# Another order of all work: r in pair loads turned on TensorE, keys of two chunks per DMA transpose, w spread by one load

## The chip, the cores and the metric

The kernel runs on one core of one Trainium2 chip. The metric is the device time of one execution in microseconds. The engines are called as in the profile: PE (TensorE, with PEld for its weight loads), DVE (VectorE), ACT (ScalarE), POOL (GpSimd) and SP (SyncE, which here only issues DMAs).

## The reference

An RWKV-5 style linear attention, followed by a layer norm and a feed-forward block with a residual. Shapes: batch 4, 8 heads, 768 tokens, head size 48; after attention the heads are put side by side to 384 channels, and the feed-forward is 384 to 1536 to 384.

```
for t in range(S):                       # per batch and head
    cur   = outer(u * k[t], v[t])
    y[t]  = r[t] @ (state + cur)
    state = w[:, None] * state + outer(k[t], v[t])
x   = y with the heads side by side       # (4, 768, 384)
xn  = (x - mean(x)) / sqrt(var(x) + 1e-6) * g_ln
out = x + relu(xn @ w_ch1) @ w_ch2
```

## The kernel before

**Tiling.** The 4 x 768 tokens are 24 chunks of 128 tokens, six to a batch. A chunk's attention is done in matrix form: keys are multiplied by a falling power of w (`Fk`) and queries by a rising one (`Fr`), so that `AT` (scores), a mask `AM`, `Y` (output) and `S` (state update, and the u term through q = r times k) are matmuls. The powers are exponentials of position times log w. `ZU`/`ZD` carry the state from chunk to chunk. The feed-forward (`UP`, `RL`, `DN`, `OT`) is matmuls of 128 channels with weights kept in SBUF; chunks are taken in the `GROUPS` of one or two.

**Layout.** Chunks 0 to 3 are loaded as two pairs: partition p then holds tokens 2p and 2p+1 of 256 tokens, and the pair steps (`LK2`, `LR2`, `LV2`, `SK2`, `SR2`, `AT2`, `AM2`, `Q2`, `CC2`, `VB2`, `Y2`) work on both. Chunks 4 to 23 are loaded one by one (`LK`, `LR`, `LV`) and use the plain steps. `AT` needs k and r with the channels on partitions, so every chunk's scaled k and r (tile `sc`) is turned: on PE through one PSUM bank named `tr` and an eviction (`TR`, `TC`) for chunks 0 to 7, by DMA transposes on SP (`TD`) for chunks 8 to 23. The normed x is turned on PE (`LT`, `XT`) for groups 0 to 7 and by DMA (`LTD`) for groups 8 to 17.

**Order.** Nothing is scheduled automatically. A hand-kept list, `PLAN`, names every step with its index and its engine (v DVE, s ACT, g POOL, - for PE or SP); each engine takes its instructions in this order, and waits where its operand is not ready. PSUM has one bank (or pair of banks) each for `tr`, `at`, `s`, `y` and `o`, and two named `hp` for `UP`. `RL` evicts `hp` on ACT or DVE.

**Steps that matter here.** `WF` loads w as a row, `LN` takes its logarithm, `WBM` spreads it over 128 partitions by a matmul, `FK2`, `FR2`, `FK`, `FR` are exponentials from it. `ROWS` loads u and w a second time by channel, for `UW` and `WL`. `DU` issues matmuls on a zero tile. `TL` is one line:

```
nc.scalar.preload_act_table_set("natural_log_exp_and_others")
```

`RS` computes 1/sqrt(variance) of a group: on ACT as Ln and then Exp, on POOL with a power. `SQ`, the squares, precedes it on ACT. In `PLAN` of before, `TL,0,s` stands among the first steps, ahead of `LN`; nine `RS` are on ACT and nine on POOL.

Of the kernel before, what the change touches and what calls it, by code (L numbers as in the profile page):

```python
# [14 lines left out]
ZPE = [1, 2, 3, 4]  # L15
SLOTS = {'kf': 8, 'rf': 8, 'vf': 10, 'sc': 6, 'vv': 6, 'trs': 6, 'q': 3, 'A': 3, 'cc': 6, 'Z': 4, 'ZS': 3, 'Vb': 4, 'x': 12, 'xn': 3, 'xT': 4, 'hT': 4, 'ot': 4}
PAIRS = 2
PLAN = """
MW,0,v LG,0,s LR,4,- MO,0,v MP,3,g MI2,0,g MZ,0,v ROWS,3,s WF,0,- LK2,1,- MP,4,g ROWS,1,s MM,0,g LK2,0,- TL,0,s MP,1,g MP,0,g MI,0,g LR2,0,- MM2,0,g
LN,0,s UGC,0,s ROWS,2,s DU,3504,- WBM,0,- ROWS,0,s LV2,0,- FK2,0,s LR2,1,- FK2,1,s FR2,1,s SK2,0,v FR2,0,s LV2,1,- SR2,0,v DU,4832,- TRk2,0,- TCk2,0,v LK,4,- UW,0,g  # L20
MP,2,v DU,1936,- TRr2,0,- SK2,1,v TCr2,0,s LR,5,- SR2,1,v CV2,0,s DU,2736,- AT2,1,- Q2,0,v LW1,2,- TRr2,1,- CV2,1,s AM2,1,v S,0,- LW1,1,- WL,0,s TCr2,1,v DU,704,-
AT2,0,- LK,5,- FK,0,s CC2,0,v ZU,0,v LV,4,- TRk2,1,- FR,0,s AM2,0,v S,1,- TCk2,1,s VB2,0,v DU,816,- Y2,0,- Q2,1,v AT2,2,- X,0,v SW,6,s SW,7,g AM2,2,v
SW,8,s DU,656,- Y2,1,- SR,4,g XN,0,s LK,6,- ZU,1,v SK,4,g LT,0,- S,2,- XT,0,v SW,4,s LW1,0,- MP,5,v X,1,v SQ,0,s SK,5,g AT2,3,- ZU,2,v LR,6,-
# [36 lines left out]


@with_exitstack
def kernel(
    ctx: ExitStack,
    tc: tile.TileContext,
    r: bass.AP,
    k: bass.AP,
    v: bass.AP,
    w: bass.AP,
    u: bass.AP,  # L70
# [187 lines left out]
    def MP(i, e):  # L258
        engines[e].memset(sc(i)[:, :, :, D:DP], 0.0)
# [525 lines left out]
```

## Time and profile before

| What | Value |
|---|---|
| median of 3 runs | 155.34 us (155.19 to 159.82) |
| profiled execution, its span | 155.5 us |
| PE busy | 143.6 us (92%) |
| DVE busy | 119.8 us (77%) |
| ACT busy | 78.7 us (51%) |
| POOL busy | 71.4 us (46%) |
| DMA queue of SP, share of 16 engines | 83.4% |

Busy times add up the instructions of an engine. An engine that is busy for most of the span can be the one that paces the kernel, but only a look at stretches and at waits says where. The granted TensorE clock is 0.998 of full speed in the mean. A row of a view of groups gives the busy time and the mean duration of one instruction, then the idle time ahead of the group and what ended it.

### The profile page before, as it was taken

The page shows a single profiled execution, that of the slowest core. Times are in us where ns is not written, and L with a number is a line of the kernel's source. Part 1 is how long each engine was busy: PE and PEld are TensorE (multiplying, and loading weights), DVE is VectorE, ACT ScalarE, POOL GpSimd, SP SyncE. Part 2 cuts the span into 40 slices and gives each one's busy share as a digit, 9 for nine tenths or more (in the row PEclk, how much of TensorE's full clock was granted, in tenths as well). Part 3 has the DMA queues.
Part 4 walks back from the last instruction along what each step waited for, and adds up shares of the span by engine and source line. Part 5 has one row for each costly group of instructions (what it writes and reads, how often), then busy time and mean ns, then how long its engine had stood idle before and what let it go on. Part 6 is the DMA issues. An engine that isn't in the chain of part 4 may idle for free.

```text
span 155.5 us, 4587 instructions
## 1 busy us (share of the span) xinstructions
PE 143.6 (92%) x1872; PEld 110.4 (71%) x1872; DVE 119.8 (77%) x229; ACT 78.7 (51%) x178; POOL 71.4 (46%) x109
## 2 busy tenths in 40 slices
PE   6989999989899868999999799899999799999991
PEld 2347888877776856788777578586777587868881
DVE  2289998549979769999995996899867539998532
ACT  3629678584361507539734457446066372146510
POOL 7220759481525547844589455332024413431500
PEclk9999999999999999999999999999999999999999
DMA  4999999998789999769999999899999998661503
GB/s 85 301 314 299 268 251 181 169 208 175 149 110 188 183 211 227 155 127 226 152 223 209 129 208 226 149 206 211 118 250 196 117 262 158 177 146 30 177 27 125
DMA packets 98486, 28.48 MB, mean 183 GB/s; under 512 B 93729, under 2 KB 96930, under 8 KB 98466
## 3 DMA queue, kind: packets, MB, share of 16 engines
q1 hardware_dynamic: 96802, 27.01, 83.4%
q0 software_dynamic: 432, 1.18, 4.1%
q8 instruction: 14, 0.23, 0.6%
q10 hardware_dynamic: 1232, 0.00, 0.4%
q14 instruction: 6, 0.05, 0.1%
HBM read 18.88 MB, written 4.72 MB: 152 GB/s over the span
## 4 chain that ended last, share of the span: by engine, by line
PE 41%; DMA 27%; DVE 12%; SPq 9%; issue 5%; POOL 3%; ACT 1%; DVEq 0%; POOLq 0%; ACTq 0%
PE o L676 17%; PE hp L648 17%; DMA trs<-sc 9%; DMA kf<-in_k_dram 5%; DMA w_sb<-in_moe_w_ch_dram 5%; DMA xT<-xn 3%; DVE Vb L567 3%; SPq L337 2%; DVE A L517 2%; DMA out_dram<-ot 2%; DMA rf<-in_r_dram 2%; SPq L356 2%; PE at L507 2%; POOL q L196 1%; DVE q L196 1%
## 5 line engine op out<-in xcount | busy, mean ns | idle before, releaser
L648 PE MATMUL hp<-xT,w_sb 128*128 128x128 bf16 (+1 forms) x648 | 56.1, 238 | 2.4 <-DMA xT<-xn 0.9
L648 PEld LDWEIGHTS <-w_sb 128*128 128x128 bf16 x648 | 48.8, 114 | 6.7 <-issue 2.7
L664 ACT ACTIVATE hT<-hp 128x512 bf16<-128x512 f32 x55 | 32.3, 592 | 41.7 <-PE hp L648 41.3
L676 PE MATMUL o<-w_sb,hT 128*128 128x384 bf16 x276 | 52.6, 326 | 0.6 <-DMA w_sb<-in_moe_w_ch_dram 0.4
L676 PEld LDWEIGHTS <-hT 128*128 128x128 bf16 x276 | 25.0, 97 | 13.9 <-issue 0.7
L517 DVE TENSOR_TENSOR A<-at,mask 128x1024 bf16<-128x1024 f32 x20 | 24.3, 1216 | 1.1 <-PE at L507 1.0
L608 POOL TENSOR_SCALAR xn<-x,sm 128x384 bf16<-128x384 f32 x14 | 9.0, 646 | 24.9 <-DVE x L592 16.1
L732 DVE SCALAR_TENSOR_TENSOR ot<-o,rs,x 128x384 f32<-128x384 f32 x23 | 14.1, 613 | 6.6 <-PE o L676 5.4
L196 POOL TENSOR_TENSOR sc<-kf,Fk 128x384 bf16<-128x384 f32 x14 | 15.3, 1100 | 4.7 <-DMA kf<-in_k_dram 4.7
L599 ACT ACTIVATE sqj<-x,sm 128x384 bf16<-128x384 f32 x24 | 14.6, 610 | 3.9 <-DVE x L592 3.8
L196 POOL TENSOR_TENSOR sc<-rf,Fr 128x384 bf16<-128x384 f32 x10 | 10.4, 1042 | 12.1 <-DMA rf<-in_r_dram 12.1
L592 DVE SCALAR_TENSOR_TENSOR x<-y,Vb 128x384 f32<-128x384 f32 x24 | 13.2, 550 | 2.4 <-POOL Vb L567 1.3
L666 DVE TENSOR_SCALAR hT<-hp 128x512 bf16<-128x512 f32 x17 | 11.5, 685 | 2.5 <-PE hp L648 2.4
L567 DVE TENSOR_TENSOR Vb<-vf,cc 128x384 f32<-128x384 f32 x13 | 11.4, 875 | 0.5 <-ACT cc L191 0.4
L196 POOL TENSOR_TENSOR q<-trs 128x512 bf16<-128x512 bf16 x8 | 9.4, 1170 | 3.4 <-DMA trs<-sc 1.8
L196 DVE TENSOR_TENSOR sc<-rf,Fr 128x384 bf16<-128x384 f32 (+1 forms) x12 | 8.2, 683 | 2.9 <-DMA rf<-in_r_dram 2.9
L196 DVE TENSOR_TENSOR sc<-kf,Fk 128x384 bf16<-128x384 f32 (+1 forms) x8 | 6.2, 780 | 5.1 <-DMA kf<-in_k_dram 5.1
L507 PE MATMUL at<-trs 48*128 48x128 bf16 x160 | 8.0, 219 | 2.3 <-DMA trs<-sc 2.3
L567 POOL TENSOR_TENSOR Vb<-vf,cc 128x384 f32<-128x384 f32 x7 | 5.8, 828 | 9.1 <-DVE cc L193 5.3
L271 PE MATMUL o<-warm 128*128 128x512 bf16 x26 | 8.1, 439 | 1.2 <-DVE u_p L210 1.2
L191 ACT CAST vv<-vf 128x384 bf16<-128x384 f32 (+1 forms) x15 | 8.1, 550 | 1.9 <-DMA vf<-in_v_dram 1.9
L507 PEld LDWEIGHTS <-trs 48*128 48x128 bf16 x160 | 4.5, 94 | 6.2 <-DMA trs<-sc 2.9
(98 smaller groups left out, 189.1 us busy)
## 6 DMA issues: line engine op xcount, KB each, us to landing
out_dram<-ot SPq DMA_DIRECT2D x23, 192.0 KB, 2.9
rf<-in_r_dram SPq DMA_DIRECT2D x20, 192.0 KB, 4.0
kf<-in_k_dram SPq DMA_DIRECT2D x20, 192.0 KB, 4.2
vf<-in_v_dram SPq DMA_DIRECT2D x20, 192.0 KB, 4.0
w_f<-in_moe_w_ch_dram SPq DMA_DIRECT2D x3, 768.0 KB, 6.0
w_sb<-in_moe_w_ch_dram POOLq DMA_DIRECT2D x3, 384.0 KB, 7.6
kf<-in_k_dram SPq DMA_DIRECT2D x2, 384.0 KB, 4.1
rf<-in_r_dram SPq DMA_DIRECT2D x2, 384.0 KB, 4.4
```

The source lines that it names most:

```text
L196: engines[e].tensor_tensor(out=out, in0=in0, in1=in1, op=ALU.mult)
L507: nc.tensor.matmul(out=t[:, par, q, :], lhsT=trs(i)[p0 : p0 + D, 1, q, :], rhs=trs(i)[p0 : p0 + D, 0, q, :], start=True, stop=True,)
L517: nc.vector.tensor_tensor(out=AA(i)[:, a:b].rearrange("p e q t -> p (e q) t"), in0=psum["at", i][:, a:b].rearrange("p e q t -> p (e q) t") ...
L567: engines[e].tensor_tensor(out=heads(Vb(i)), in0=vf(i), in1=cc(i)[:].unsqueeze(2).to_broadcast([P, H, D]), op=ALU.mult,)
L592: nc.vector.scalar_tensor_tensor(out=xx(i)[:], in0=psum["y", i][:, :C], scalar=1.0, in1=Vb(i), op0=ALU.mult, op1=ALU.add, accum_out=sm[i][:],)
L599: nc.scalar.activation(out=sqj[:], in_=xx(i)[:], func=ACT.Square, bias=sm[i][:], scale=-float(C), accum_out=sq[g][:, j : j + 1])
L608: engines[e].tensor_scalar(out=xn(g)[:, j], in0=xx(i)[:], scalar1=-float(C), scalar2=sm[i][:], op0=ALU.mult, op1=ALU.add)
L648: nc.tensor.matmul(out=t[:, a * gw : (a + 1) * gw], lhsT=w1_sb[n][kc][:, fb::FB], rhs=xT(g)[:, :size, kc, :], start=(kc == 0), stop=(kc == ...
L664: nc.scalar.activation(out=o, in_=s, func=ACT.Relu)
L666: nc.vector.tensor_relu(out=o, in_=s)
L676: nc.tensor.matmul(out=psum["o", i][:, :C], lhsT=hT(g)[:, fk, j * P : (j + 1) * P], rhs=w2_sb[d][:, a, :], start=(fk == 0), stop=(fk == FK ...
L732: nc.vector.scalar_tensor_tensor(out=ot(i)[:], in0=psum["o", i][:, :C], scalar=rs[g][:, j : j + 1], in1=xx(i)[:], op0=ALU.mult, op1=ALU.add,)
```

## The change

- **r of chunks 4 to 17** is loaded by seven pair loads (`LR2`), scaled two chunks at a time (`SR2`) and turned on PE (`TRr`). Its eviction `TCr` puts the tokens back in order, in two copies of 128 x 512. r of chunks 18 to 23 is loaded by chunk and turned by DMA (`TDr`).
- **k** is still loaded by chunk from chunk 4 on. Two chunks share a tile `sk`; it is turned on PE (`TRk`) for chunks 4 to 9 and by one DMA transpose for two chunks (`TDk`) for chunks 10 to 23. A DMA transpose has the same size as before; there are ten instead of sixteen.
- **For all chunks** `CV`, `Q`, `CC` and `VB` now do two chunks at a time (`CV2`, `Q2`, `CC2`, `VB2`); the u term of both is made in the even chunk's `S`.
- **w** is loaded by one DMA that repeats the row on 128 partitions. `LN` works on all of them; `WBM` and the four `ROWS` are gone. u comes as a row (`UF`), `UWR` multiplies it by w, and `COL` turns log w and u times w into columns by 16 small matmuls.
- **`Y2`** alternates the two halves of the partitions from matmul to matmul.
- **`PLAN`** is written anew. Engines of some steps change: for instance `RL` on ACT 55 to 50, `XN` on POOL 14 to 10, seven of eight `SR2` on POOL. `DU` has 12576 columns instead of 15280. `TL,0,s` now stands behind `DN,61`, after `RS` 0, 2, 5, 7, 6 and 9 on ACT; `RS` 14, 13 and 15 on ACT stand behind it.

Core of the diff:

```diff
     def WF(i, e):
-        queues[e].dma_start(out=w_row[:], in_=w.rearrange("h d -> (h d)").rearrange("(o c) -> o c", o=1))
+        queues[e].dma_start(out=w_bc[:], in_=bass.AP(tensor=w.tensor, offset=w.offset, ap=[[0, P], [1, C]]))
...
     def LN(i, e):
-        nc.scalar.activation(out=ln_row[:], in_=w_row[:], func=ACT.Ln)
-
-    def WBM(i, e):
-        t = psum["wb"] = ps.tile([P, 512], FP32, name="y")
-        nc.tensor.matmul(out=t[:, :C], lhsT=ones[:], rhs=ln_row[:], start=True, stop=True)
-        psum["ln"] = t[:, :C].rearrange("p (h d) -> p h d", h=H)
+        nc.scalar.activation(out=ln_bc[:], in_=heads(w_bc[:]), func=ACT.Ln)
...
+    def COL(i, e):
+        t = psum["col"] = ps.tile([P, 2, HP], FP32, name="y")
+        src = (ln_bc[0:1].rearrange("p h d -> p (h d)"), uw_row[:])
+        for j in range(2):
+            for h in range(H):
+                q, par = divmod(h, 2)
+                nc.tensor.matmul(
+                    out=t[par * DP : par * DP + D, j, q : q + 1], lhsT=src[j][:, h * D : (h + 1) * D], rhs=one[:],
+                    start=True, stop=True,
+                )
...
+    def SKH(i, e):
+        g, x = divmod(i, 2)
+        times(e, sk(g)[:, x, :, :D], slots(kf2(g))[:, x], Fk2[:, x])
...
+    def TCr(g, e):
+        o, t = trr(g)[:], psum["tr", g][:]
+        if g < PAIRS:
+            copy(e, o.rearrange("p a q t -> p (a q) t"), t)
+        else:
+            for a in range(2):
+                copy(
+                    e, o[:, a].rearrange("p q (t x) -> p x q t", x=2),
+                    t[:, :, a * LH : (a + 1) * LH].rearrange("p (x q) t -> p x q t", x=2),
+                )
+
+    def TDk(g, e):
+        queues[e].dma_start_transpose(
+            out=trk(g)[:].rearrange("p a q t -> p (a q) t"), in_=sk(g)[:].rearrange("p a h d -> p (a h d)")
+        )
...
     def Y2(i, e):
...
+        for q in range(HP):
+            for a in range(2):
+                h0 = a * LH
+                if (2 * g + a) % NCH > 0:
+                    add(a, t[h0 : h0 + LH, q * E2 : (q + 1) * E2], trr(g)[:, jt, q, h0 : h0 + LH], ZZ(2 * g + a - 1)[:, q, :])
+        for js in range(2):
+            for par in range(2):
                 for q in range(HP):
...
+                    h = 2 * q + par
+                    for a in range(2):
+                        h0 = a * LH
+                        add(
+                            a, t[h0 : h0 + LH, h * D : (h + 1) * D],
+                            AA(2 * g + js)[h0 : h0 + LH, par, q, jt * LH : (jt + 1) * LH], vals[h0 : h0 + LH, h, js, :],
                         )
...
     def SR(i, e):
-        times(e, sc(i)[:, 0, :, :D], rf(i), Fr[:])
+        times(e, sr(i // 2)[:, i % 2, :, :D], rf(i), Fr[:])
```

The new `PLAN` where the first and the third `RS` on ACT stand, and where `TL` stands:

```
... RL,16,v RL,32,s Y,4,- TCk,3,v SW,8,s UP,33,- LR2,4,- CC2,2,v SW,6,v AT,5,- RL,33,s LT,3,- VB2,2,g
UP,2,- AM,5,v RS,0,s UP,18,- RL,2,s XT,3,v AT,6,- IW2,2,g X,4,v RL,18,s UP,34,- ...
... UP,80,- RL,81,s AM,9,v TRr,5,- RS,5,s LR2,7,- S,9,- SR2,6,g DN,16,- TCr,5,s X,8,v UP,98,- SQ,6,s STO,1,-
DN,17,- RL,80,s SK,13,v LT,7,- DN,18,- SQ,8,s ZD,8,v LV,10,- Q2,5,g UP,96,- ...
... XN,18,v UP,194,- RL,195,s LTD,13,- DN,61,- TL,0,s RL,194,v DN,62,- ...
```

More of the change, by code (lines that the diff above doesn't have):

```diff
@@ L20 @@
[L20 to L23, printed above, removed]
@@ new lines @@
+LV2,0,- FK2,0,s SKH,1,v FR2,0,s MO,0,v MP,1,v SKH,0,g MP,5,v MZ,0,v LG,0,s LK,5,- FK,0,s SRH,0,v TRk,0,- FR2,1,s MP,2,v
+MP,3,g DU,1760,- UWR,0,v TCk,0,s LR2,2,- SRH,1,v SK2,1,v TRr,0,- LW1,0,- DU,1472,- TCr,0,v SR2,1,g LV2,1,- AT2,0,- TRk,1,- CV2,0,s
+LK,4,- AM2,0,v COL,0,- TCk,1,s Q2,0,v AT2,1,- WL,0,s TRr,1,- UW,0,v AM2,1,v LW1,1,- S,0,- SR2,2,g TCr,1,s DU,1504,- ZU,0,v
+UGC,0,s AT2,2,- CC2,0,s LR2,3,- Y2,0,- AM2,2,v VB2,0,g SW,2,s S,1,- LK,6,- DU,640,- SK,5,g X,0,v TRr,2,- CV2,1,s ZU,1,v
+AT2,3,- XN,0,g Y2,1,- LV,4,- TCr,2,s Q2,1,v SW,1,v SW,0,s LT,0,- AM2,3,v SK,4,g S,2,- XT,0,s UP,0,- CC2,1,s ZU,2,v
@@ new lines @@
+LV,5,- SW,5,s SW,3,g TRk,2,- X,1,v S,3,- SW,4,s TCk,2,v LK,7,- XN,1,s SR2,3,g ZU,3,v UP,1,- SQ,1,s RL,0,v LW1,2,-
+LT,1,- Y2,2,- LV,7,- XT,1,s VB2,1,v LV,6,- TRr,3,- SK,6,g X,2,v UP,17,- TCr,3,s Y2,3,- XN,2,v RL,17,s Q2,2,v RL,1,s
+CV2,2,g LK,9,- LT,2,- AT,4,- XT,2,s UP,16,- SK,7,v IW2,0,g SQ,0,s UP,32,- X,3,v IW2,1,g AM,4,v XN,3,s S,4,- SQ,2,s
+TRk,3,- LK,8,- SW,7,g RL,16,v RL,32,s Y,4,- TCk,3,v SW,8,s UP,33,- LR2,4,- CC2,2,v SW,6,v AT,5,- RL,33,s LT,3,- VB2,2,g
+UP,2,- AM,5,v RS,0,s UP,18,- RL,2,s XT,3,v AT,6,- IW2,2,g X,4,v RL,18,s UP,34,- ZU,4,v XN,4,g UP,50,- AM,6,v RL,34,s
@@ new lines @@
+RS,1,g Y,5,- CV2,3,s UP,49,- X,5,v SQ,3,s AT,7,- Q2,3,v LT,4,- Y,6,- RL,50,s DN,0,- AM,7,v RS,3,g SQ,5,s UP,48,-
+LV,8,- XT,4,s S,6,- XN,5,v FR,0,s DN,1,- CC2,3,v RL,49,s ZU,6,v VB2,3,g DN,2,- RL,48,v LV,9,- S,7,- UP,64,- OT,0,v
+SK,9,g ZU,7,v DN,4,- X,6,v LK,11,- DN,5,- SK,8,g DN,6,- SR2,4,g LR2,5,- TRk,4,- OT,1,v UP,66,- TCk,4,s Y,7,- RL,66,v
+LK,12,- DN,8,- RS,2,s CV2,4,g X,7,v TRr,4,- RL,64,v LK,10,- DN,9,- TCr,4,s ZD,7,v DN,10,- SK,11,v SQ,4,s UP,65,- Q2,4,v
+LR2,6,- SQ,7,s LT,5,- OT,2,v AT,8,- S,8,- AM,8,v XN,6,s LV,11,- DN,12,- SK,12,g XT,5,s DN,13,- LK,15,- RL,65,v XN,7,g
@@ new lines @@
+SK,17,g DN,32,- STO,6,- CV2,7,s STO,5,- DN,33,- SK,16,v LK,18,- SQ,12,s UP,149,- X,13,v ZU,13,v AT,15,- XN,13,g RL,149,s UP,146,-
+XN,12,v UP,147,- ZD,13,v LTD,10,- RL,146,s SR2,8,g DN,34,- S,14,- LK,21,- OT,8,v UP,145,- CC2,7,s SQ,13,s RL,147,v LV,17,- DN,36,-
+VB2,7,g ZU,14,v TRr,8,- AM,15,v Y,14,- UP,144,- ZD,14,g TDk,8,- X,14,v DN,37,- RL,144,s RL,145,v S,15,- SQ,10,s Y,15,- SK,18,v
+DN,38,- ZU,15,v SQ,11,s STO,7,- SK,21,g UP,148,- OT,9,v LV,16,- UP,165,- X,15,v STO,8,- XN,14,g RL,148,s DN,40,- TCr,8,s ZD,15,v
@@ L300, in UW @@
             p0 = par * DP
-            times("g", uwI[p0 : p0 + D, :, par], u_p[p0 : p0 + D, :], w_p[p0 : p0 + D, :])
+            copy(e, uwI[p0 : p0 + D, :, par], psum["col"][p0 : p0 + D, 1, :])
     def WL(i, e):
-        nc.scalar.activation(out=ln_p[:], in_=w_p[:], func=ACT.Ln)
         for par in range(2):
@@ L744 @@
     steps = dict(
-        MI2=MI2, MM2=MM2, FK2=FK2, FR2=FR2, LK2=LK2, LR2=LR2, LV2=LV2, SK2=SK2, SR2=SR2, CV2=CV2, TRk2=TRk2, TRr2=TRr2,
-        TCk2=TCk2, TCr2=TCr2, Q2=Q2, AT2=AT2, AM2=AM2, CC2=CC2, VB2=VB2, Y2=Y2,
-        WF=WF, LG=LG, UGC=UGC, WBM=WBM, MO=MO, LW1=LW1, SW=SW, ROWS=ROWS, MW=MW, TL=TL, MI=MI, MM=MM, MP=MP, MZ=MZ, DU=DU, LN=LN, FK=FK_, FR=FR_, UW=UW, WL=WL,
-        IW2=IW2, LK=LK, LR=LR, LV=LV, SK=SK, SR=SR, CV=CV, TR=TR, TC=TC,
-        TD=TD, Q=Q, AT=AT, AM=AM, S=S_, CC=CC, ZU=ZU, ZD=ZD, VB=VB, Y=Y, X=X, SQ=SQ, XN=XN,
-        RS=RS, LT=LT, LTD=LTD, XT=XT, UP=UP, RL=RL, DN=DN, OT=OT, STO=STO, DA=DA, DB=DB, OA=OA, OB=OB, SA=SA, SB=SB,
+        MW=MW, MO=MO, MZ=MZ, MI=MI, MI2=MI2, MM=MM, MM2=MM2, MP=MP, TL=TL, DU=DU, WF=WF, UF=UF, LG=LG, UGC=UGC,
+        LN=LN, FK=FK_, FR=FR_, FK2=FK2, FR2=FR2, UWR=UWR, COL=COL, UW=UW, WL=WL, LW1=LW1, SW=SW, IW2=IW2,
+        LK=LK, LR=LR, LV=LV, LK2=LK2, LR2=LR2, LV2=LV2, SK=SK, SR=SR, SK2=SK2, SR2=SR2, SKH=SKH, SRH=SRH, CV2=CV2,
+        TRk=TRk, TRr=TRr, TCk=TCk, TCr=TCr, TDk=TDk, TDr=TDr, Q2=Q2, AT2=AT2, AT=AT, AM2=AM2, AM=AM, S=S_, CC2=CC2,
+        ZU=ZU, ZD=ZD, VB2=VB2, Y2=Y2, Y=Y, X=X, SQ=SQ, XN=XN, RS=RS, LT=LT, LTD=LTD, XT=XT, UP=UP, RL=RL, DN=DN,
+        OT=OT, STO=STO, DA=DA, DB=DB, OA=OA, OB=OB, SA=SA, SB=SB,
     )
```

293 lines of the change are left out of this document (119 added, 174 removed).

## Prediction

> **What bounds the kernel now.** I read the page's busy shares first, then busy time by stretch, then the waits of TensorE (PE), then the groups and the chain for durations.
>
> ```profile
> span 155.5 us, 4587 instructions
> ...
> PE 143.6 (92%) x1872; PEld 110.4 (71%) x1872; DVE 119.8 (77%) x229; ACT 78.7 (51%) x178; POOL 71.4 (46%) x109
> ...
> q1 hardware_dynamic: 96802, 27.01, 83.4%
> ```
>
> ```profile
> 0.00:20.00 20.00, 17.74 (x224) 10.46 (x224) 12.98 (x27) 11.91 (x21) 8.44 (x29) 1.00 0.95 249
> 20.00:152.00 132.00, 125.55 (x1647) 99.83 (x1647) 106.23 (x202) 66.81 (x158) 62.95 (x81) 1.00 0.89 176
> ```
>
> The columns are the stretch and its length, then busy time of PE, its weight loads, DVE, ACT and POOL, the granted clock and the DMA share. From 20 to 152 us PE is busy 125.55 of 132 us at the full granted clock: it paces the kernel, and only 6.4 us there are idle. So a change moves the time in three ways only: PE work added or removed after 20 us, PE waits added or removed, and how early the first `UP` comes. The present waits:
>
> ```profile
> PE at L507 <- DMA trs<-sc: 2.3, 3, 1.7
> ...
> PE s L535 <- DVE q L196: 1.2, 1, 1.2
> ...
> PE hp L648 <- DMA xT<-xn: 0.9, 1, 0.9
> ...
> PE hp L648 <- ACT hT L664: 0.7, 1, 0.7
> ```
>
> They come to 5.1 us, in total, times and longest. 3.2 us of them end with a DMA transpose (`trs`, `xT`), the rest with DVE or ACT. ACT waits for PE, not PE for ACT: of `RL`'s evictions hT (L664) the groups below show 41.3 us of ACT idle until PE delivers.
>
> **The sum** is made against the profiled execution, 155.5 us, which is the median shown (155.34 us) within 0.2 us. A difference of 2% (3.1 us) is about what a measurement of this kernel can tell from no change.
>
> **1. Transposes that move to PE.** `TRk`/`TRr` do 14 turns of eight, the old `TR` family did 8: 48 more transposes, nearly all after 20 us.
>
> ```profile
> 42.86 0.45 PE tr L486 x8
> ...
> 45.28 0.17 PE tr L633 x3
> ...
> 59.22 0.71 ACT sqj L599 x2
> ...
> 61.66 0.33 PE at L507 x8
> ...
> 62.26 0.65 PE o L676 x4
> ...
> 68.78 0.19 PE s L548 x4
> 68.98 0.67 PE hp L648 x12
> 69.65 0.17 PE y L577 x4
> 69.82 0.20 PE y L585 x8
> ```
>
> Eight cost 0.45 us in the chain, so six turns are **+2.7 us**. Their evictions (`TCr` in two halves of 512 columns, about 0.58 us each on ACT, worked out from 474 ns for 384 and 1.01 us for 1024 columns below) lie on ACT and DVE beside PE; if that cover went, `TCr` would hold the one `tr` bank and the next turn or `LT` would wait for it.
>
> **2. The order inside `Y2`** now alternates the two halves of the partitions.
>
> ```profile
> 20.56 0.44 PE L390 MATMUL at<-trs,trs 48*64 48x128 bf16 x16
> 20.93 0.86 PE L648 MATMUL hp<-xT,w_sb 128*128 128x128 bf16 x12
> ...
> 22.49 0.68 PE L465 MATMUL y<-vv,A 64*64 64x48 bf16 x16
> ```
>
> Sixteen of `AT2`'s matmuls, which alternate partition halves, take 0.44 us although they stream 128 columns; sixteen of `Y2`'s, which stay in one half, take 0.68 us with 48. At the rate of `AT2` the 64 of `Y2,2` and `Y2,3` save 4 x 0.24 = 1.0 us; `Y2,0` and `Y2,1` lie in the front (step 4). **-1.0 us**; ends 0 and -1.4.
>
> **3. DMA.** Seven pair loads of r replace fourteen of one chunk, ten transposes replace sixteen, each 3.7 us from issue to landing:
>
> ```profile
> trs<-sc SPq DMA_TRANSPOSE x16, 3.7
> ```
>
> No PE wait is for `rf`. What counts is the queue: thirteen issues fewer on SP, six of them transposes. For chunks 4 to 9 neither operand of `AT` waits for a transpose any more, for 10 to 17 only the key, for 18 to 23 both as now; but a transpose of two chunks waits for the later of them, and behind it on SP wait the loads, `LTD` and `STO` that follow in the order. Of the 6.4 us idle I take off 2.0 of the 3.2 that end with a transpose, and the 1.2 for q (`Q2` does two chunks in one go, and DVE loses `CC`, `VB` and `Q` instructions): 3.2 are left, **-3.2 us**. Ends: -5 (only 1.4 us stays) and +3 (each of seven paired keys 0.4 us late more than what is saved).
>
> Edits that cost nothing by this reading: pair steps on POOL (`SR2`, `VB2`) are longer, but POOL has 84 us free; `UF`, `UWR`, `COL`, `UW` replace four small loads; `COL`'s 16 one-column matmuls stand ahead of `AT2,1`, whose result DVE takes only after `AM2,0` and `Q2,0` (1.9 us); if that cover went, up to 2 us. `TL` moved (step 5) passes no SP or POOL step.
>
> **4. The front.** Here w must reach FK2 before anything else.
>
> ```profile
> 1.23 0.47 SPq L203 DMA_DIRECT2D w_row<-in_w_dram  x1
> ...
> 2.40 1.28 ACT L225 ACT_TABLE_LOAD   x1 [2.40 <-DVE epsc L265]
> ...
> 3.72 0.52 ACT L276 ACTIVATE ln_row<-w_row 1x384 f32<-1x384 f32 x1
> ...
> 5.45 1.05 ACT L293 ACTIVATE Fk<-y,pow 128x384 f32<-128x384 f32 x2 [1.12 <-PE y L280]
> ...
> 10.52 1.01 ACT L191 COPY trs<-tr 128x1024 bf16<-128x1024 bf16 x1 [3.07 <-PE tr L486]
> ...
> 17.37 0.56 DVE L592 SCALAR_TENSOR_TENSOR x<-y,Vb 128x384 f32<-128x384 f32 x1 [0.23 <-PE y L465]
> ```
>
> Now: logarithm 3.72, spreading matmul `WBM`, FK2 from 5.45 to 6.50, x of chunk 0 done at 17.93, the first `UP` at 20.93. After: w's load is issued first on ACT's queue, half a microsecond earlier than at 1.23, and writes 128 rows, so I let it land at 3.5; LN 0.55 us, a table load of 1.28 us (step 5), FK2 1.05 us, end 6.4: `WBM`'s gain is eaten. FR2 (two more, with FK between) ends at about 8, the r turn's eviction is DVE's instead of ACT's 1.01 us, and `AT2,0` ends at about 11.1, 1 us earlier. On DVE then follow `AM2,0`, `Q2,0`, `AM2,1`, `ZU,0` (0.55 us), `AM2,2` and `X,0`:
>
> ```profile
> L592 DVE SCALAR_TENSOR_TENSOR x<-y,Vb 128x384 f32<-128x384 f32 x24 | 13.2, 550 | 2.4 <-POOL Vb L567 1.3 <-PE y L465 0.4
> ...
> L400 DVE TENSOR_TENSOR A<-at,mask 128x1024 bf16<-128x1024 f32 x4 | 4.9, 1216 | 0.0
> ...
> L196 DVE TENSOR_TENSOR q<-trs,trs 128x1024 bf16<-128x1024 bf16 x2 | 1.4, 692 | 0.0
> ```
>
> 11.1 + 3 x 1.22 + 0.69 + 2 x 0.55 = 16.6 us instead of 17.93: **-1.3 us**; without the load -2.6. Ends -3 and +1.5 (w landing 2.8 us later than I think). Fewer dummy matmuls (`DU`, 15280 to 12576 columns) only fill this stretch.
>
> **5. Where `TL` stands.** This is the largest term. `TL` loads the table set that holds logarithm and exponential together. In the order of before it runs ahead of `LN`. ACT's groups:
>
> ```profile
> L664 ACT ACTIVATE hT<-hp 128x512 bf16<-128x512 f32 x55 | 32.3, 592 | 41.7 <-PE hp L648 41.3
> ...
> L606 ACT ACTIVATE xn<-x,sm 128x384 bf16<-128x384 f32 x8 | 4.9, 615 | 3.0 <-DVE x L592 3.0
> ...
> L191 ACT COPY xT<-tr 128x384 bf16<-128x384 bf16 x4 | 1.9, 474 | 2.5 <-PE tr L633 2.5
> L191 ACT CAST vv<-vf 128x768 bf16<-128x768 f32 x2 | 1.6, 834 | 0.0
> L615 ACT ACTIVATE rs<-sq,epsc 128x1 f32<-128x1 f32 x5 | 1.5, 292 | 0.0
> L225 ACT ACT_TABLE_LOAD x1 | 1.3, 1283 | 2.4 <-DVE epsc L265 2.4
> ...
> L616 ACT ACTIVATE rs<-rs 128x1 f32<-128x1 f32 x5 | 1.0, 203 | 0.2
> ```
>
> One load of 1283 ns; every `RS` on ACT (Ln, then Exp) costs 292 + 203 ns. In the new order `TL` stands behind `DN,61`, when six such `RS` (0, 2, 5, 7, 6, 9) are through. What must stand in its place no row shows. Ends: nothing (the program settles on the joint set by itself), or one load at every change from Ln to Exp and back. I take the second, since a step naming the joint set would be idle otherwise: 2 loads in the front, 12 in the six `RS`, `TL` itself: 15 loads, 19 us of ACT instead of 1.3. Each `RS` then holds ACT 2 x 1.28 + 0.49 = 3.06 us. ACT is in order; behind `RS` stand `RL`s, and PE has two `hp` buffers, so the second `UP` after the held one waits. By the durations of steps 1 and 5, with ACT caught up ahead of `RS`, from the end of the PE step named:
>
> ```
> place    held on ACT, done at                          PE gets there       PE waits
> RS,0     from UP,33:  RL,33, RS, RL,2       4.25       UP,34   2.17        2.1
> RS,2     from TRk,4:  TCk,4, RS, TCr,4      5.23       LT,5    4.11        1.1, +0.2 for Q2,4
> RS,5     from UP,81:  RL, RS, TCr,5         4.82       LT,7    3.36        1.46
>                       then SQ,6, RL,80      6.12       UP,96   5.64        0.48
> RS,7+6   from UP,96:  X,9, SQ,9, RL,96,
>          CV2,5, RS, XN,8, RS, RL,112        10.5       UP,114  7.4         3.1
> RS,9     from UP,165: TCr,8, SQ,15, RS, RL  5.52       UP,164  2.95        2.6
> ```
>
> 11.0 us; with an `RS` of 0.49 us each of these rows ends before PE gets there. Part of it falls together with the 3.2 us of waits that step 3 left, as DMAs and DVE catch up meanwhile: I take off 1.5. **+9.5 us**; ends 0 and +11. `TL` itself, behind `RL,195`, holds nothing that PE needs soon.
>
> [...]
>
> **Sum:** 155.5 + 2.7 - 1.0 - 3.2 - 1.3 + 9.5 = **162.2 us**.
>
> **The rivals.**
> - *Doubled loads don't arise.* For it: the trace shows one load for 9 pairs and Relu, Square and copies run between them. Against: a step exists that names the set. Then 155.5 + 2.7 - 1.0 - 3.2 - 2.6 = **151.4 us**, faster. It decides at the second ACT_TABLE_LOAD.
> - *Loads are there, but ACT's slack takes most of them.* ACT has 77 us free, and where PE gets late for other reasons `RL` is in time. A third of 11.0 us: 155.5 + 2.7 - 1.0 - 3.2 - 1.3 + 3.7 = **156.4 us**. Against: PE is 95% busy and the buffers are two.
> [...]
> - *POOL's long pair steps set X.* No doubled loads, but `VB2` on POOL, twice the length below, comes late for `X` by one such length in each of seven pairs: 151.4 + 7 x 0.83 = **157 us**. Against: POOL is 46% busy.
>
> ```profile
> L567 POOL TENSOR_TENSOR Vb<-vf,cc 128x384 f32<-128x384 f32 x7 | 5.8, 828 | 9.1 <-DVE cc L193 5.3 <-ACT cc L191 2.1 <-issue 1.5
> ```
>
> **How the numbers follow.** Forecast 0.62, no doubled loads 0.12, slack 0.15, emptying 0.06, POOL 0.05. The forecast's own range is 156.5 to 168: its steps' ends added half-way. The whole range, **151.0 to 170.0**, takes in the second and third case and leaves out the lower half of the first rival and nearly all of the emptying case. Faster by over 2% (below 152.2): 0.12 x 0.7 + 0.15 x 0.15 + 0.62 x 0.04 = 0.13. Slower (above 158.4): 0.62 x 0.85 + 0.06 + 0.05 x 0.4 + 0.15 x 0.35 = 0.66. Within: 0.21.
>
> **What would show it.** Step 5: 15 ACT_TABLE_LOADs, 19 us, ACT near 97 us busy (78.7 + 14 x 1.28), and PE's waits for hT of ACT from 0.7 to 7 us or more, ahead of UP,34, UP,96, UP,114, UP,164. Step 1: 112 transposes of 56 ns. Step 2: a 16-group of `Y2` near 0.44 us. Step 3: PE's waits for `trs` under 1 us, queue q1 well below 83%. Step 4: x of chunk 0 at 16.6 us, a second load between LN and FK2. A single table load would make the forecast wrong at its root; 15 loads with PE waits under 4 us would make its table of places wrong.

## The result and the profile after

The changed kernel takes 169.54 us (median of 5, 167.35 to 175.22) where the kernel before takes 155.21 us in the same comparison: a ratio of 1.082, interval 1.073 to 1.090. A ratio leaves out executions more than 1.5% above the fastest of their kernel, so it is not the quotient of the medians. 162.2 us was forecast, in a range of 151 to 170.

The page of the kernel after, its first lines, the row of the granted clock (40 slices of the span, in tenths of full speed, 9 for 90% or more) and the row of the main DMA queue:

```profile
span 173.5 us, 4698 instructions
...
PE 152.8 (88%) x1943; PEld 118.1 (68%) x1943; DVE 113.5 (65%) x208; ACT 99.8 (58%) x192; POOL 79.2 (46%) x96
...
PEclk9978555899799969999969999999999999999999
...
q1 hardware_dynamic: 83184, 25.44, 65.8%
```

The profiled execution is the one of 175.22 us, with a mean clock of 0.921; the others have 0.96 to 0.97. So its counts, waits and landing times are used here, and sizes in us are taken from experiments at full clock where there are any.

ACT's groups of the kernel after, the rows of table loads (busy time, mean ns of one):

```profile
L609 ACT ACT_TABLE_LOAD x6 | 7.7, 1283 | 0.1
L610 ACT ACT_TABLE_LOAD x6 | 7.7, 1283 | 0.1
...
L276 ACT ACT_TABLE_LOAD x1 | 1.3, 1283 | 1.8 <-issue 1.8
L288 ACT ACT_TABLE_LOAD x1 | 1.3, 1283 | 0.1
L224 ACT ACT_TABLE_LOAD x1 | 1.3, 1283 | 0.0
```

L609 and L610 are Ln and Exp of `RS`, L276 is `LN`, L288 `FK2`, L224 `TL`: fifteen loads where there was one, in the places forecast. What PE waits for, in the kernel after (total, times, longest; L642 is `UP`, L387 the turns of k and r, L670 `DN`, L627 `LT`):

```profile
PE hp L642 <- ACT hT L658: 4.5, 2, 2.5
...
PE tr L387 <- POOL sk L202: 4.0, 1, 4.0
...
PE o L670 <- ACT hT L658: 3.7, 1, 3.7
...
PE tr L627 <- ACT trr L197: 3.1, 2, 1.8
```

Three of the four are waits for ACT, 11.3 us together; the fourth, 4.0 us, is in the front. No wait for a DMA transpose is left. The busy times by stretch of the kernel after, columns as in the prediction; 27.85 us is the start of the first `UP` (20.93 before) and 170.31 us the end of PE's work:

```profile
0.00:12.00 12.00, 6.55 (x32) 3.04 (x33) 4.32 (x16) 6.74 (x9) 4.74 (x22) 0.96 0.85 193
12.00:20.00 8.00, 7.54 (x125) 4.63 (x123) 5.07 (x8) 4.30 (x8) 4.38 (x3) 0.71 0.89 234
20.00:32.00 12.00, 12.00 (x173) 9.52 (x170) 7.98 (x13) 5.73 (x11) 9.34 (x11) 0.52 1.01 260
...
27.85:170.31 142.46, 130.89 (x1664) 104.49 (x1663) 98.18 (x177) 85.50 (x170) 63.68 (x67) 0.95 0.69 146
```

And the same stretch, first `UP` to the end of PE's work, of the kernel before:

```profile
20.93:152.34 131.41, 124.96 (x1630) 99.29 (x1624) 105.50 (x198) 66.24 (x156) 62.09 (x80) 1.00 0.89 176
```

This splits the 18.0 us between the two spans. The first `UP` is 6.9 us later. Behind it PE idles 11.6 us instead of 6.45 (142.46 - 130.89 against 131.41 - 124.96), 5.1 us more, and is busy 5.9 us longer. What follows PE's last matmul is 3.2 us in both.

One `RS` in ACT's timeline of the kernel after (start, length):

```profile
39.80 0.60 ACT L658 ACTIVATE hT<-hp 128x512 bf16<-128x512 f32 x1 [0.53 <-PE hp L642]
40.42 1.28 ACT L609 ACT_TABLE_LOAD   x1
41.71 0.29 ACT L609 ACTIVATE rs<-sq,epsc 128x1 f32<-128x1 f32 x1
42.02 1.28 ACT L610 ACT_TABLE_LOAD   x1
43.32 0.20 ACT L610 ACTIVATE rs<-rs 128x1 f32<-128x1 f32 x1
43.43 1.07 ACT L658 ACTIVATE hT<-hp 128x512 bf16<-128x512 f32 x2
```

Ln and Exp are 0.5 us of work and hold ACT for 3.1 us. PE's timeline shows the second `UP` behind it starting late:

```profile
44.06 1.77 PE L642 MATMUL hp<-xT,w_sb 128*128 128x128 bf16 x24 [2.02 <-ACT hT L658]
```

### The profile page after: what moved, and what is told of

The parts are those of the page before. It is cut to its first block, busy times and chain, and to the rows that moved or that the text cites. A ratio compares the mean times of both kernels' runs of the same rounds, so it can differ in the third digit from the quotient of the medians.

```text
span 173.5 us, 4698 instructions
## 1 busy us (share of the span) xinstructions
PE 152.8 (88%) x1943; PEld 118.1 (68%) x1943; DVE 113.5 (65%) x208; ACT 99.8 (58%) x192; POOL 79.2 (46%) x96
## 4 chain that ended last, share of the span: by engine, by line
PE 71%; ACT 19%; DMA 3%; issue 2%; DVE 2%; POOL 1%; ACTq 0%; POOLq 0%; DVEq 0%
PE hp L642 26%; PE o L670 23%; ACT L610 4%; ACT L609 4%; PE tr L387 3%; PE s L477 3%; PE at L540 3%; DMA w_bc<-in_w_dram 3%; PE y L500 3%; ACT hT L658 3%; ACT trr L197 2%; PE y L579 2%; PE y L571 2%; PE s L456 1%; PE o L271 1%
## 5 line engine op out<-in xcount | busy, mean ns | idle before, releaser
L642 PE MATMUL hp<-xT,w_sb 128*128 128x128 bf16 (+1 forms) x648 | 59.4, 244 | 4.6 <-ACT hT L658 4.5
L670 PE MATMUL o<-w_sb,hT 128*128 128x384 bf16 x276 | 54.5, 334 | 3.7 <-ACT hT L658 3.7
L642 PEld LDWEIGHTS <-w_sb 128*128 128x128 bf16 x648 | 51.3, 116 | 8.7 <-issue 4.9
L670 PEld LDWEIGHTS <-hT 128*128 128x128 bf16 x276 | 25.5, 99 | 17.5 <-ACT hT L658 4.1
L488 POOL TENSOR_TENSOR Vb<-vf,cc 128x768 f32<-128x768 f32 x9 | 13.6, 1515 | 30.5 <-DVE cc L199 20.1
L202 POOL TENSOR_TENSOR sr<-rf,Fr 128x768 bf16<-128x768 f32 (+1 forms) x10 | 17.1, 1707 | 2.6 <-DMA rf<-in_r_dram 2.6
L202 POOL TENSOR_TENSOR sk<-kf,Fk 128x384 bf16<-128x384 f32 x12 | 12.6, 1051 | 5.8 <-ACT Fk L288 4.9
L197 ACT COPY trr<-tr 128x512 bf16<-128x512 bf16 (+1 forms) x13 | 9.0, 756 | 4.9 <-PE tr L387 4.9
L202 POOL TENSOR_TENSOR q<-trk,trr 128x1024 bf16<-128x1024 bf16 x4 | 8.5, 2128 | 6.7 <-ACT trr L197 6.7
L202 DVE TENSOR_TENSOR sk<-kf,Fk 128x384 bf16<-128x384 f32 (+1 forms) x11 | 6.5, 587 | 6.8 <-ACT Fk L288 6.8
L197 ACT CAST vv<-vf 128x768 bf16<-128x768 f32 x9 | 7.5, 829 | 4.8 <-DMA vf<-in_v_dram 4.8
L202 POOL TENSOR_TENSOR Z<-ZS,WLZ 128x384 bf16<-128x384 f32 x6 | 6.3, 1047 | 7.8 <-DVE ZS L561 7.8
L477 PE MATMUL s<-vv,sk 128*128 128x96 bf16 (+1 forms) x96 | 8.3, 223 | 0.0
L540 PE MATMUL at<-trr,trk 48*128 48x128 bf16 x160 | 8.3, 227 | 0.0
```

Of the source, the lines that this page charges most:

```text
L197: nc.scalar.copy(out=out, in_=in_)
L202: engines[e].tensor_tensor(out=out, in0=in0, in1=in1, op=ALU.mult)
L477: nc.tensor.matmul(out=t[:, q * E2 : (q + 1) * E2].rearrange("p (e d) -> p e d", e=2), lhsT=lhs, rhs=rhs, start=first, stop=True, skip_gro ...
L488: engines[e].tensor_tensor(out=Vb2(g).rearrange("p (x h d) -> p x h d", x=2, h=H), in0=vals, in1=cc2(g)[:].unsqueeze(3).to_broadcast([P, 2 ...
L540: nc.tensor.matmul(out=t[:, par, q, :], lhsT=trk(g)[p0 : p0 + D, a, q, :], rhs=trr(g)[p0 : p0 + D, a, q, :], start=True, stop=True,)
L642: nc.tensor.matmul(out=t[:, a * gw : (a + 1) * gw], lhsT=w1_sb[n][kc][:, fb::FB], rhs=xT(g)[:, :size, kc, :], start=(kc == 0), stop=(kc == ...
```

## The experiments

The theory: the loads at `RS` cost some 11 us of PE's waits, and the rest is the front, where w comes late, PE runs dry and its clock falls. Rivals: the new order itself, or the way of r and k, is slower; a load holds ACT for longer than its 1.28 us; the fall of the clock alone does it all. In the expectations T stands for the loads and F for the front and the clock. "As changed" below means the kernel after.

### a_tl_first, b_tl_behind_wl: one table load, or three

```diff
- ... RL,195,s LTD,13,- DN,61,- TL,0,s RL,194,v ...
+ ... RL,195,s LTD,13,- DN,61,- RL,194,v ...
  a:
- ... UF,0,s ...
+ ... UF,0,s TL,0,s ...
  b:
- ... WL,0,s ...
+ ... WL,0,s TL,0,s ...
```

> The changed kernel with TL moved ahead of LN again: one table load instead of fifteen, all else as changed. Theory T (the table loads are the loss): the five waits of PE behind RS (2.0 + 1.3 + 1.75 + 3.7 + 2.5 = 11.3 us in the changed kernel's trace) go, and 1.3 us in the front; with a fast run of the changed kernel near 167.5 us that leaves 152 to 156 us, PE's waits for ACT under 2 us. Theory F (the front and the clock are the loss: w's spread load lands at 5.6 us, PE idles and its granted clock falls to 0.5 from 20 to 32 us): the loads cost little, 162 to 166 us, clock as low in the front as before.

> The changed kernel with TL directly behind WL: three table loads, all in the front; the twelve at RS are gone. Theory T: the loads at RS go (11.3 us), the one between LN and FK2 stays, so 1.3 us more than with TL ahead of LN, 154 to 157 us. Theory F: that one load adds to the late w and to the clock's fall, 3 us or more above the kernel with TL ahead of LN.

a: 155.79 us, ratio 0.998 (0.992 to 1.004) to the kernel before. b: 155.1 us, ratio 1.006 (1.001 to 1.011). So nearly the whole 8% hangs on the place of one line; the other parts of the change neither gain nor lose together. The two loads more in b's front come to 0.8 of a per cent by these ratios, but the intervals still overlap and the medians order the two the other way; in the profiles b's first `UP` starts 1.7 us after a's (24.02 us against 22.33). a from first `UP` to the end:

```profile
22.33:148.40 126.07, 124.77 (x1665) 100.25 (x1663) 101.35 (x178) 68.82 (x157) 67.66 (x69) 1.00 0.82 172
```

PE idles 1.3 us of 126.

### k_loads_at_rs: the loads put back, without those of the front

```diff
  on top of a:
+    def TX(i, e):
+        nc.scalar.preload_act_table_set("exp_and_others")
...
- ... WL,0,s ...
+ ... WL,0,s TX,0,s ...
- ... DN,61,- RL,194,v ...
+ ... DN,61,- TL,0,s RL,194,v ...
```

> The changed kernel with TL ahead of LN, but with the set for exponentials alone preloaded behind WL and the joint set again behind DN,61: the front has one load ahead of LN, the six RS have their twelve. If the loss at the RS is what the sum of PE's waits says (11.3 us), 11 to 14 us above the kernel with TL ahead of LN, so 165 to 169 us, nearly all of the changed kernel's loss. If the front is the larger part, 157 to 161 us.

172.58 us, the median of 164.57, 172.33, 172.83 and 190.04, so above the 165 to 169 expected; the profiled execution is the fastest, with a clock of 0.99 like a's. Its stretch from first `UP` to the end, and PE's waits:

```profile
22.15:159.68 137.53, 126.25 (x1665) 101.07 (x1663) 98.58 (x177) 85.38 (x170) 67.39 (x69) 0.99 0.72 157
```

```profile
PE hp L645 <- ACT hT L661: 4.5, 2, 2.5
PE o L673 <- ACT hT L661: 3.7, 1, 3.7
PE tr L630 <- ACT trr L197: 2.9, 2, 1.5
```

At equal clock the stretch is 11.5 us longer than a's: 10.0 us more idle (11.3 against 1.3) and 1.5 us more busy, the latter with the clock. The waits sit in the same places and have nearly the same size as in the kernel after. This settles the first part of the theory: the twelve loads at six `RS` are enough to give these waits, and without them, in a, none of these waits is over 0.2 us. The other three executions are 8 to 25 us slower at clocks of 0.93 and 0.75; why is not shown.

### d_before_tl_late, d2_before_tl_front: the same line moved in the kernel before

```diff
  both, in the kernel before: TL,0,s taken out ahead of LN
  d:
- ... DN,61,- ...
+ ... DN,61,- TL,0,s ...
  d2:
- ... FR,0,s ...
+ ... FR,0,s TL,0,s ...
```

> The kernel before with TL moved behind DN,61, nothing else: 17 table loads, six RS on ACT (2, 4, 6, 7, 10, 11) with two each. Theory T: each holds ACT 2.6 us longer and PE waits 1 to 2.5 us at most of them, plus 1.3 us in the front: 163 to 168 us. Theory F, by which the loads hide in ACT's slack: 155 to 159 us.

> The kernel before with TL moved behind the last exponential of the front (FR): five loads, all in the front, none at RS. If the front's loads cost only their own waits, 2.6 us for w's powers and the state factor: 157 to 159 us. If the idle stretch they make lets the clock fall to half as it did with TL late (20 to 32 us at 0.50), 161 to 166 us.

d: 173.51 us, ratio 1.126 (1.117 to 1.135), above the range expected. d2: 166.35 us median (161.46 to 166.7). So moving `TL` alone, in the old order, costs more than the whole change. d has 17 loads, twelve of them at `RS`; d2 has five, all in the front. Their fronts have three (d) and four (d2) loads more than before, 3.8 and 5.1 us of ACT, and in both the first `UP` came some 7 us late (27.63 and 28.14 us). d's stretches:

```profile
12.00:20.00 8.00, 5.37 (x89) 3.67 (x89) 5.48 (x9) 7.90 (x12) 2.59 (x3) 0.86 1.03 285
20.00:32.00 12.00, 12.00 (x167) 9.81 (x165) 7.68 (x14) 4.68 (x10) 7.08 (x11) 0.50 0.90 193
...
27.63:168.30 140.67, 130.20 (x1628) 103.94 (x1624) 101.43 (x198) 82.30 (x167) 60.48 (x79) 0.95 0.79 152
```

The same stretch of d2:

```profile
28.14:162.00 133.86, 129.75 (x1628) 104.03 (x1624) 100.74 (x199) 65.74 (x154) 60.70 (x79) 0.95 0.83 160
```

In d two of these loads, at 13.4 and 14.9 us, stand ahead of the state's factor on ACT, which is done only at 16.93 us. PE is dry for 2.6 us in both kernels (`s` L422 waits for `Z` on DVE, in d until 17.58 us), and its clock is at half from 17.8 to 41.7 us in d and from 18.8 to past 42 in d2, while PE is busy nearly all the time. The loads at `RS` are worth 6.8 us in this order (140.67 - 133.86), against 11.5 in the new one: what a held ACT costs depends on the order around it.

### e_fill, f_tl_first_fill: does more filling keep the clock up?

```diff
- ... DU,7200,- ...
+ ... DU,15700,- ...        # e: as changed otherwise
+ ... DU,12000,- ...        # f: on top of a
```

> The changed kernel with more dummy matmuls at the start (7200 to 15700 columns), which run while PE waits for the late w; all fifteen table loads stay. The wait itself is not shortened. If PE's idle stretch of 4 us makes the granted clock fall to half afterwards, the clock holds at 0.98 or more up to 40 us, the slowest runs vanish, and the median comes down by 3 to 8 us to 160 to 165 us. If the clock falls for another reason, it is the same as the changed kernel, 167 to 170 us.

> The changed kernel with TL ahead of LN and 12000 columns of dummies instead of 7200, so that PE has work until about when the first transpose can start. If the row load of w gained its 2 to 3 us by keeping PE busy (its FK2 began only 0.17 us earlier), this kernel gains the same: 151.5 to 153 us, clock 0.995. If it gained by w itself, this one stays at 154.5 to 156 us.

e: 168.69 us, ratio 1.077 (1.066 to 1.087): no cure, as its four executions have clocks of 0.99, 0.98, 0.97 and 0.93. Its profiled execution, the one of 0.99, shows the kernel after with a front at full clock (1.00 in every stretch up to 32 us; its time is 165.75 us, so the fall of the clock alone is not the loss); its row of the granted clock, and the stretch behind the first `UP`:

```profile
PEclk9999999999999999998799999999999999999999
```

```profile
23.36:160.86 137.50, 126.24 (x1665) 101.01 (x1663) 98.12 (x178) 85.34 (x170) 67.01 (x69) 0.99 0.73 155
```

The dip lies in slices 19 and 20, from 73.8 to 82.0 us; in the kernel after the longest of the waits for ACT, the 3.7 us at `RS,7` and `RS,6`, ended at 85.6 us and the clock fell to half at 86.1. f: 155.01 us, its executions two at 1.0 and two at 0.96; 153.2 us in the first pair, 156.9 in the second. That is how far the time goes with the clock from one execution to the next, with a single table load. Its median lies in the range expected if w itself were the gain of c below; the pair at full clock, 153.0 and 153.4 us, lies at the upper edge of the other range.

### c_tl_first_w_row, i_best, j_best_w_bc: w by one row

```diff
  c, on top of a:
-        queues[e].dma_start(out=w_bc[:], in_=bass.AP(tensor=w.tensor, offset=w.offset, ap=[[0, P], [1, C]]))
+        queues[e].dma_start(out=w_row[:], in_=w.rearrange("h d -> (h d)").rearrange("(o c) -> o c", o=1))
...
+    def WBM(i, e):
+        nc.tensor.matmul(out=t[:, :C], lhsT=ones[:], rhs=ln_row[:], start=True, stop=True)
...
- ... LN,0,s ... DU,7200,- ...
+ ... LN,0,s DU,3504,- WBM,0,- DU,3696,- ...
- ... FR2,1,s ... FR,0,s ...
+ ... FR2,1,s FR,0,s ...
  i, on top of c: the second DU has 2900 columns
  j, on top of a: DU,7200 becomes DU,11000
```

> The changed kernel with TL ahead of LN and w loaded as one row and spread by a matmul as in the kernel before (FR moved up behind FR2, since it reads the matmul's bank). Theory T: FK2 ends at 6.5 us instead of 7.3, so 0.5 to 1 us below the kernel with TL ahead of LN alone. Theory F: w lands by 3.7 us, PE's idle stretch ahead of the first transposes shrinks by 1 us or more and the clock holds in the front: 3 to 5 us below it.

> The changed kernel with TL ahead of LN and w as a row spread by a matmul, as already run, with 800 columns of dummies less, so that the first transpose starts when its operand is ready (8.15 us instead of 8.80): 0.97 to 0.985 of the kernel before, 0 to 0.7 us below that run.

> The changed kernel with w by one spreading load, TL ahead of LN, and 11000 columns of dummies. The only difference left to the kernel with w's row is w's path. If the row's gain was PE kept busy, the two are within 0.5 us; if w's earlier landing counts, this one is 1 to 2 us slower.

c: 151.99 us, ratio 0.984 (0.978 to 0.991). i: 152.26 us, 0.986 (0.980 to 0.993), six executions at clocks of 0.989 to 0.999. j, with w still repeated on 128 partitions: 153.95 us, 0.992 (0.987 to 0.997), twelve executions at 0.955 to 1.0. So c and i beat both kernels, by 1.4% for i; both intervals lie below 1, but a gain of 2% is not shown. By the medians the row is better than the repeated load. j's interval overlaps i's, but at clocks of 0.999 or 1.0 i's three executions took 151.6 to 152.0 us and j's six 152.4 to 154.1. So the row's way gains something at equal clock too, though not by which step is shown; and i's clock was 0.989 or more in every execution. i's first `UP` starts at 21.57 us, a's at 22.33. i's clock, and its stretch behind the first `UP`:

```profile
PEclk9999999999999999999999999999999999999999
```

```profile
21.57:146.68 125.11, 124.14 (x1665) 100.10 (x1663) 101.36 (x178) 68.27 (x156) 67.98 (x69) 1.00 0.82 168
```

### g_y2_old, h_keys_dma: two parts undone in i

```diff
  g: Y2 in the order of before
-        for q in range(HP):
-            for a in range(2):
+        for a in range(2):
+            for q in range(HP):
...
  h: keys of chunks 6 to 9 by DMA
- TRk,3,-  TCk,3  TRk,4,-  TCk,4
+ TDk,3,-         TDk,4,-
```

> As the kernel with TL ahead of LN and w's row, but Y2 in the old order (one half of the partitions after the other). By the prediction's step 2, 1.0 us slower, 2 at most if Y2,0 and Y2,1 count too; by the traces, where 40 matmuls of a Y2 take 0.9 instead of 1.8 us, 1.8 to 3.6 us slower. If Y2 hides behind DVE in the front, no difference.

> As the kernel with TL ahead of LN and w's row, but the keys of chunks 6 to 9 turned by DMA (two TDk for two TRk with their evictions). By step 1 each turn on PE costs 0.45 us, so 0.9 us faster if the DMA's 3.2 us hide. If AT,6, which comes about 3.3 us of PE work behind TRk,3, then waits for the DMA, 1 to 4 us slower: the turn on PE is the cheaper one in the front.

g: 159.19 us, ratio 1.031 (1.025 to 1.037), far more than expected. `Y2`'s matmuls of the two kernels, first g, then i, from PE's groups by shape:

```profile
L507 PE MATMUL y<-vv,A 64*64 64x48 bf16 x128 | 6.9, 206 | 0.0
```

```profile
L507 PE MATMUL y<-vv,A 64*64 64x48 bf16 x128 | 2.7, 187 | 0.0
```

Part of that is the clock, which is at half in g from 15.0 to 28.7 us and puts its first `UP` at 26.44 us:

```profile
PEclk9999555899999999999999999999999999999999
```

The kernel before, at full clock and in the same order as g:

```profile
L465 PE MATMUL y<-vv,A 64*64 64x48 bf16 x128 | 5.4, 187 | 0.0
```

So the order is worth 2.7 us of PE work, about half of it ahead of the first `UP`. The clock is not shown to fall through `Y2`. PE's timeline of g, then of i, at the five dummy matmuls behind `WBM` and at the last `AT2` ahead of the first `Y2`:

```profile
5.31 1.25 PE L273 MATMUL o<-warm 128*128 128x512 bf16 x5
...
16.36 0.66 PE L437 MATMUL at<-trr,trk 48*64 48x128 bf16 x16
16.79 1.04 PE L507 MATMUL y<-vv,A 64*64 64x48 bf16 x16
```

```profile
5.79 2.31 PE L273 MATMUL o<-warm 128*128 128x512 bf16 x5
...
16.21 0.44 PE L437 MATMUL at<-trr,trk 48*64 48x128 bf16 x16
```

In g the sixteen matmuls are slow already, before any `Y2` has run. And the two profiles differ from 5 us on, where i's dummies are the slow ones, at 0.46 us each against 0.25, although the view shows a clock of 1.00 for both. So g's dummies ran out earlier, and PE then waited 1.0 us for `sk`. All six executions of g have a clock of 0.957, i's have 0.989 or 0.999, with the same steps up to there; why, stays open.

h: 155.88 us, ratio 0.993 (0.983 to 1.004). PE's waits of h:

```profile
PE at L547 <- DMA trk<-sk: 3.5, 1, 3.5
```

Two turns on PE (0.9 us of matmuls) are replaced by one wait of 3.5 us. So the turn of these keys on PE is worth its time. The interval overlaps i's; the wait is plain, and h's clock has a mean of 0.94 from 32 to 90 us, where i's has 1.00.

## Why the prediction was right, and where its steps were not

The sum came from PE's path, and near full clock that path is measured: e's profile, a span of 164.0 us, against 155.5 before. By the same division as above:

| | forecast | e |
|---|---|---|
| first `UP` (step 4) | -1.3 | +2.4 |
| PE busy behind it (steps 1, 2) | +1.7 | +1.3, with 1.5 of lower clock (e against a) |
| PE idle behind it (steps 3, 5) | +6.3 | +4.8 |
| sum | 162.2 | 164.0 |

Spans and times must be kept apart: every time in the comparisons is about 1.8 us longer than the span of its execution. So e's 164.0 us belong to a time of 165.75. And the span of 155.5 us, which the prediction took for the same as the median time of 155.34, belongs to an execution some 2 us slower than that median. In times the change cost 14.3 us (169.54 against 155.21) where 6.9 were forecast (162.2 against 155.34). The median lies 3.8 us above e's time and 7.3 above the forecast. The executions above e's fastest have lower clocks, 0.92 to 0.98 in e and in the kernel after, and no step of the prediction had the clock.

**Step 5, the table loads: right**, in mechanism, places and size. Waits of 2.0 and 2.5 us (`hp`), 1.3 and 1.8 (`tr`) and 3.7 (`o`) stand against 2.1, 2.6, 1.3, 1.94 and 3.1 in the table of places; at `RS,7` and `RS,6` it was a `DN` that waited, not `UP,114`. Sum 11.3 against 11.0. ACT is busy 99.8 us against 97. Behind the overlap that the forecast took off, 9.5 us were left; in k the idle grew by 10.0 us against a. The rival *no doubled loads* fell with fifteen loads; *slack takes most* with those 10.0 us; *POOL's pair steps set X* fell with a, whose PE idles only 1.3 us. No run shows ACT emptied by a load, the case that has 0.06 in the chances: in the timeline 0.01 to 0.02 us lie between a load and its neighbours, and each `RS` holds ACT for the 3.1 us that two loads of 1.28 us and its 0.5 us of work come to.

**Step 4, the front: wrong.** The failed number is "I let it land at 3.5". The chain of waits of the kernel after:

```profile
0.72 4.90 DMA w_bc<-in_w_dram
...
5.64 0.53 ACT ln_bc L276
...
6.25 0.51 ACT L288
...
7.54 1.13 ACT Fk L288 x2
```

w landed at 5.6 us, so `FK2` ended at 8.7 instead of 6.4. Of the tile x, the view from 18 to 24 us has the step that writes it, of 558 ns, and its start:

```profile
L586 DVE SCALAR_TENSOR_TENSOR x<-y,Vb x1: 558/558/558, 21.6 to 21.6; 128x384 f32<-128x384 f32 x1
```

x of chunk 0 was done at 22.2 us instead of 16.6. The end given for this, +1.5 us, held only the delay. What the delay did to PE was no part of it: the `DU` that was called mere filling ran out at 5.85 us, and PE waited 4.0 us for `sk`. Then its clock fell twice, as short stretches show:

```profile
12.00:14.00 2.00, 2.00 (x21) 0.94 (x23) 0.79 (x2) 0.83 (x1) 1.76 (x1) 0.50 0.93 234
14.00:16.00 2.00, 1.95 (x66) 1.69 (x62) 1.43 (x2) 0.98 (x2) 1.44 (x1) 0.90 0.87 261
...
18.00:20.00 2.00, 2.00 (x22) 0.73 (x20) 0.91 (x2) 0.79 (x2) 0.81 (x1) 0.50 0.66 127
```

In stretches of 0.25 us, half clock lasts from 11.0 to 14.4 us and again from 17.8 to 31.5. The first fall is behind the wait of 4.0 us; ahead of the second, long one PE had been at full clock again and had no wait above 0.5 us, so that the late w caused it is not shown. With one table load and w by a row the first `UP` is still at 21.57 us, 0.6 later than before: the new front is no gain in any version tried.

**Step 3, DMA waits: right in kind, its size not shown.** In a PE's idle time behind the first `UP` falls from 6.45 to 1.3 us, which would be the lower end (-5) and not the -3.2 taken. But the 6.45 us are those of one execution. Its span of 155.5 us is 2.6 us longer than the median, 152.9, of the eighteen executions of the kernel before that ran at a clock of 0.999 or 1.0 in the later comparisons, and against those a is no faster (ratio 0.998). Which waits those eighteen had, no profile shows; gains that this section takes against the profile before may be that much too large, and losses that much too small. The pairs' later operands, the reason for caution, cost nothing that the waits show.

**Steps 1 and 2, PE work: wrong in sign.** +1.7 forecast, -0.8 measured in i (124.14 against 124.96). Eight transposes take 0.45 us, as said. But `Y2` gains more: a block of 40 matmuls took 1.80 us in g at full clock and 0.91 in i, twice behind the first `UP`, -1.8 instead of -1.0, as the matmuls with the state gain too (eight of them take 0.36 us in i, four in g). And one part was not costed: the u term's small matmuls. Before and i, from PE's groups by shape:

```profile
L535 PE MATMUL s<-uwI,q 128*128 128x2 bf16 x80 | 4.9, 165 | 1.2 <-DVE q L196 1.2
...
L416 PE MATMUL s<-uwI,q 128*128 128x2 bf16 x16 | 0.7, 164 | 0.0
```

```profile
L463 PE MATMUL s<-uwI,q 128*128 128x2 bf16 x96 | 4.1, 164 | 0.2 <-DVE uwI L200 0.2
```

96 matmuls in both, 5.6 us and 4.1: now that the u term of two chunks is made at one place they cost 1.5 us less. No run undoes this part alone.

The misses in steps 1, 2 and 3 made the forecast too slow, the one in step 4 and the missing clock made it too fast. So the forecast of slower was right for its main reason, while the nearness of its sum to e's span of 164.0 us is in part luck.

**What stays open** is the clock. It fell behind long waits of PE (4.0 and 3.7 us in the kernel after, 2.6 in d), but also without one: in the kernel after at 17.8 us, and in g, whose longest wait once PE has begun is 1.0 us. And it differs between executions of one kernel.

## What to carry to other kernels

Where a step that names a table set is moved, list every activation that comes to stand ahead of it, count the loads, and price each by what waits behind it on ACT: twelve loads cost 11.5 us in one order and 6.8 in another. What the first step of a front needs is judged by when it lands among the other loads, not by when it is issued (w in the kernel after: issued at 0.7 us, landed at 5.6). Where a delay lets PE run dry, a fall of its clock is to be looked for (in d behind 2.6 us without work, at half from 17.8 to 41.7 us), which costs time beside the wait (f: 153.2 us at a clock of 1.0, 156.9 at 0.96); with filling alone (e, f) executions still had clocks of 0.93 and 0.96. And a profile is one execution: before a gain is read from it, its span is set beside the times of the others.

## What the runs showed of the hardware

- A clock that has fallen can stay down under full work: in the kernel after PE is busy 12.00 of 12 us from 20 to 32 us at 0.52, in d 12.00 of 12 at 0.50. The fall lasts 13.7 us in the kernel after (17.8 to 31.5) and 23.9 in d; the other four falls of the kernel after (from 11.0, 45.1, 62.2 and 86.1 us) last 3.4 us each. The waits ahead of the falls differ as well: in the kernel after 4.0 us, ending at 9.9 us, ahead of the fall at 11.0, 1.3 us, ending at 60.7 us, ahead of the one at 62.2, and at 17.8 us none above 0.5 us since its last rise. In a the wait was 2.3 us; behind it eight transposes took 1.04 us (0.62 for the eight from 12.93 us on), at a mean clock of 0.86 over the first 12 us.
- One row of 1536 bytes repeated on 128 partitions took 4.9 us to land among the first loads of k and r. Loaded once, in c, it was issued at 0.7 us too, and `LN` started on it at 2.8 us without waiting for it.
- Every one of the 15 table loads took 1283 ns, and 0.01 to 0.02 us lay between a load and its neighbours in the timeline above.
- In the first microseconds the view's clock did not tell the speed: at 1.00 in both, the same five dummy matmuls took 1.25 us in g and 2.31 in i.
- Matmuls of 64 x 64 that alternate the halves of the partitions took half the time of those that stay in one: 2.7 us against 5.4 for 128.
